# 144 unread products on 128, 64 and 32 rows behind TensorE's last product

## The chip, the cores and the metric

One core of a Trainium2 chip runs the whole kernel. The metric is the device time of one execution in microseconds. Engines are called TensorE (PE in the profile, PEld for its weight loads), VectorE (DVE), ScalarE (ACT), GpSimd (POOL) and SyncE (SP, which issues all DMAs here).

## What is computed

The reference takes x (8 x 4160 tokens of 192 numbers) through a light convolution and then through a maxout layer:

```python
w = softmax(weight_gen)                      # per token and head, 7 taps, 8 heads
x = sum over k of w[.., k] * x_pad[t + k]    # 24 columns per head
h = maximum(maximum(x @ w1, x @ w2), x @ w3) # 192 -> 768
out = h @ w_out                              # 768 -> 192
```

All is float32, and the output has 33280 rows of 192.

## The kernel before, in words

The 33280 tokens lie as 128 partitions of 260 tokens; a chunk is 4 tokens of each partition (`TC = 4`, so `CH = 512` columns on TensorE), and there are `NC = 65` chunks. For each chunk GpSimd multiplies windows of x by the softmaxed taps (`product`, line 234), VectorE adds the taps (line 263), the sums are transposed so that the 192 features lie on partitions, and `parts` (lines 311 to 328) splits them into float32r parts: `xa_hi` and `xa_lo` for the first 128 features, `xb` and `xc` for the rest. They are kept in `state["xT", c]`. The weights are split in the same way and stay in SBUF: `wa_hi`, `wa_lo`, `wb_hi`, `wb_lo`, and `wo` for the second layer.

Every product of the two layers is issued by `product_of` (line 339), at line 343. It contracts 64 rows at a time, one half of the partitions (`halves`), so that TensorE works with two row groups of 64 rows. `up` makes the upper products, 512 columns each, into a bank `ph`; `maximum` reads the bank (lines 392 and 396) and makes `h_hi` and `h_lo`. `down` multiplies `h_hi` by 384 and `h_lo` by 192 columns of `wo`, and lines 425 and 426 add the two parts of the sum into `o`.

The order is written out: a loop over chunks and 22 ticks gives the lower half's products with `lower`, and `advance_upper` puts the upper half's products between them by a count of column slots (`SLOTS`, `clock`). `plan` is a heap of later steps with the tick at which they are due. Every instruction goes through `pin`, which keeps the program's order on its engine. In the last round (`c == NC`) the second layer of the last chunk is all that is left: its sums for four tokens lie in four banks, each is finished in turn, added (`add`, line 424) and sent out alone by SyncE (line 430). Banks come from the pool `ps`: 8 buffers, each of 128 x 512 float32, handed out in turn; whoever asks for one waits for the readers of the tile that had it before.

`busy` (line 244) puts transposes into a bank that nothing reads: `k6` and `k2` in the opening make 48 of them.

The program ends with the loop over what is left in `plan`; the change adds one call behind it.

Of the kernel before, what the change touches and what calls it, by code (L numbers as in the profile page):

```python
# [13 lines left out]
F32 = mybir.dt.float32  # L14
# [7 lines left out]
P = 128  # L22
# [63 lines left out]
def lightconv_maxout_kernel(  # L86
# [11 lines left out]
    nc = tc.nc  # L98
# [7 lines left out]
    NJ = DFF // P  # L106
# [3 lines left out]
    CH = TC * P  # L110
# [25 lines left out]
    ps = ctx.enter_context(tc.tile_pool(name="ps", bufs=8, space=bass.MemoryType.PSUM))  # L136

    ident = const.tile([P, P], F32, name="ident")
    wa_hi = const.tile([P, NJ, 3, P], F32R, name="wa_hi")
# [13 lines left out]
    state = {}  # L153
# [297 lines left out]
    def lower(task, first=0, last=None):  # L451
# [7 lines left out]
        if last is None:  # L459
            settle = SETTLE if f is down and args[0] < NC - 1 else 0.0  # L460
            begun.append((clock[0] + settle, f(*args, 1)))

    words = [w.bitcast(U32) for w in (w1, w2, w3, w_out)]


# [161 lines left out]
    NC = len(chunks)  # L627
# [70 lines left out]
    for c in range(NC + 1):  # L698
        for tick in range(TICKS):
# [10 lines left out]
            k, odd = divmod(tick - (TC if tick >= 2 * DOWN_AT else 0), 2)  # L710
# [18 lines left out]
    advance_upper(float("inf"))  # L729
    while plan:  # L730
        heapq.heappop(plan)[2]()


# [32 lines left out]
```

## Time and profile before

| what | value |
|---|---|
| median of the runs | 1677.51 us (2 runs, 1677.51 to 1677.52) |
| span of the profiled execution, first to last instruction | 1676.7 us |
| TensorE products in it | 16930 |
| last product starts | 1673.22 us |
| granted TensorE clock over the span | 1.000 |

The profiled execution's own time is known by its span; the runs' median lies 0.8 us above it. Times in the rows are microseconds from the span's start. In a timeline a row that merges several instructions gives the start of the first, the time until the end of the last and their number (x2); products overlap, so the distance between starts is the pace, and a row's own length is not.

### The profile page before, as it was taken

The numbers are of one execution on the slowest core, as the hardware profiler recorded it, in microseconds if no ns is written. First come the engines' busy times: TensorE is split into PE (matmuls) and PEld (weight loads), VectorE is DVE, ScalarE is ACT, GpSimd is POOL, SyncE is SP. The second block draws the span as 40 slices with busy tenths as digits, with TensorE's granted clock in tenths as the row PEclk, the third lists the DMA queues.
The fourth block names the chain that finished last, engine by engine and source line by source line (L and its number), as shares of the span: only waits on it lengthen the run. The fifth ranks groups of instructions, "written<-read, shape, count | busy, mean of one in ns | idle before, by whom it ended". The sixth has DMA issues, their size and how long they took to land.

```text
span 1676.7 us, 42376 instructions
## 1 busy us (share of the span) xinstructions
PE 1663.2 (99%) x16930; PEld 1654.6 (99%) x16930; DVE 1106.3 (66%) x1508; ACT 1140.5 (68%) x2880; POOL 1405.2 (84%) x823
## 2 busy tenths in 40 slices
PE   7999999999999999999999999999999999999999
PEld 6999999999999999999999999999999999999999
DVE  7866666666666666666666666666666666666653
ACT  6666676676676676676676676676676676676672
POOL 7867888888898888888898888888898888888872
PEclk9999999999999999999999999999999999999999
DMA  7010101011010101011010101011010101010000
GB/s 267 11 61 21 71 11 71 36 46 71 20 62 21 71 11 71 29 53 71 20 62 20 71 11 71 23 59 71 20 62 20 71 11 71 20 61 20 21 11 30
DMA packets 20278, 79.53 MB, mean 47 GB/s; under 512 B 2296, under 2 KB 4984, under 8 KB 17392
## 3 DMA queue, kind: packets, MB, share of 16 engines
q1 hardware_dynamic: 20080, 76.83, 12.1%
q8 instruction: 132, 2.16, 0.5%
q14 instruction: 66, 0.54, 0.1%
HBM read 51.26 MB, written 25.56 MB: 46 GB/s over the span
## 4 chain that ended last, share of the span: by engine, by line
PE 98%; DMA 0%; DVE 0%; SPq 0%; POOL 0%; issue 0%; ACT 0%; DVEq 0%; POOLq 0%
PE ph L343 98%; PE ph L286 0%; DMA xt<-in_x_dram 0%; SPq L575 0%; DMA h_lo<-in_moe_w_dram 0%; POOL r L234 0%; DVE ph L518 0%; DVE ph L502 0%; PE ph L248 0%; DVE ph L525 0%; SPq L566 0%; DVE wa_lo L542 0%; ACT wa_hi L539 0%; POOL wt L205 0%; DVE w L525 0%
## 5 line engine op out<-in xcount | busy, mean ns | idle before, releaser
L234 POOL TENSOR_TENSOR r<-xt,wt 128x1344 f32<-128x1344 f32 x260 | 721.1, 2817 | 1.7 <-DMA xt<-in_x_dram 1.0
L396 DVE TENSOR_TENSOR m<-ph,m 128x512 f32<-128x512 f32 x768 | 513.0, 685 | 200.5 <-PE ph L343 113.0
L401 POOL TENSOR_TENSOR h_lo<-m,h_hi 128x512 fp32r<-128x512 f32 x378 | 488.3, 1304 | 163.9 <-ACT h_hi L399 159.2
L343 PE MATMUL ph<-xa_hi,wa_hi 64*128 64x512 f32 x2340 | 621.7, 388 | 0.0
L343 PE MATMUL ph<-xb,wb_hi 64*128 64x512 f32 x2340 | 619.8, 386 | 0.2 <-ACT xb L326 0.2
L343 PE MATMUL ph<-xa_lo,wa_hi 64*128 64x512 f32 x2340 | 619.8, 386 | 0.0
L343 PE MATMUL ph<-xa_hi,wa_lo 64*128 64x512 f32 x2340 | 619.8, 386 | 0.0
L343 PE MATMUL ph<-wo,h_hi 64*128 64x384 f32 x3120 | 590.4, 355 | 0.0
L343 PE MATMUL ph<-wo,h_lo 64*128 64x192 f32 x3120 | 550.5, 247 | 0.0
L399 ACT CAST h_hi<-m 128x512 fp32r<-128x512 f32 x378 | 234.5, 621 | 403.7 <-DVE m L396 400.7
L343 PEld LDWEIGHTS ph<-wo,h_lo 64*128 64x128 f32 x3120 | 479.3, 188 | 0.0
L343 PEld LDWEIGHTS ph<-wo,h_hi 64*128 64x128 f32 x3120 | 472.1, 184 | 0.0
L263 DVE TENSOR_REDUCE acc<-r 128x192 f32<-128x1344 f32 x252 | 389.7, 1547 | 122.2 <-POOL r L234 122.2
L308 ACT COPY room<-room 32x128 f32<-32x128 f32 x1512 | 447.9, 296 | 24.6 <-DVE room L302 6.2
L343 PE MATMUL ph<-xc,wb_lo 64*128 64x512 f32 x1170 | 451.6, 386 | 0.0
L343 PEld LDWEIGHTS ph<-xa_hi,wa_hi 64*128 64x128 f32 x2340 | 358.7, 184 | 1.6 <-issue 0.4
L343 PEld LDWEIGHTS ph<-xb,wb_hi 64*128 64x128 f32 x2340 | 356.5, 184 | 1.7 <-ACT xb L326 0.5
L343 PEld LDWEIGHTS ph<-xa_lo,wa_hi 64*128 64x128 f32 x2340 | 356.7, 184 | 1.2 <-DVE xa_lo L322 0.2
L343 PEld LDWEIGHTS ph<-xa_hi,wa_lo 64*128 64x128 f32 x2340 | 356.5, 184 | 1.4 <-issue 0.2
L392 ACT COPY m<-ph 128x512 f32<-128x512 f32 x390 | 222.0, 587 | 40.0 <-PE ph L343 35.1
L426 DVE TENSOR_TENSOR o<-ph,ob 128x192 f32<-128x192 f32 x260 | 86.5, 353 | 228.8 <-ACT ob L425 228.8
L343 PEld LDWEIGHTS ph<-xc,wb_lo 64*128 64x128 f32 x1170 | 215.3, 184 | 0.6
(74 smaller groups left out, 719.2 us busy)
## 6 DMA issues: line engine op xcount, KB each, us to landing
xt<-in_x_dram SPq DMA_DIRECT2D x20, 1728.0 KB, 6.9
out_dram<-o SPq DMA_DIRECT2D x64, 384.0 KB, 2.3
wt<-in_weight_gen_dram SPq DMA_DIRECT2D x21, 336.0 KB, 3.0
xt<-in_x_dram SPq DMA_DIRECT2D x2, 960.0 KB, 6.6
h_hi<-in_moe_w_dram SPq DMA_DIRECT2D x6, 256.0 KB, 6.3
room<-in_moe_w_out_dram SPq DMA_DIRECT2D x1, 1152.0 KB, 10.6
xt<-in_x_dram SPq DMA_DIRECT2D x1, 1152.0 KB, 5.4
h_lo<-in_moe_w_dram SPq DMA_DIRECT2D x6, 128.0 KB, 4.6
```

Source lines behind the costliest of these rows:

```text
L234: eng.tensor_tensor(to, xt[:, la + t : la + t + K].rearrange("p k (h g) -> p k h g", g=G), w.rearrange("p (h k) -> p k h", k=K) .unsqueeze ...
L263: nc.vector.tensor_reduce(state["acc", c][:, t], r, axis=AX.X, op=ALU.add)
L308: pin(nc.scalar.copy(to[:, :, p : p + 32], blocks[p : p + 32, :, f : f + 32]))
L343: ins = nc.tensor.matmul(ph[:, :n], w[h], v[h], start=begins and half == 0 and q == 0, stop=ends and half == 1 and q == len(terms) - 1,)
L392: pin(nc.scalar.copy(m, ph))
L396: pin(nc.vector.tensor_tensor(to, ph, m, op=ALU.max))
L399: later(1, lambda: pin(nc.scalar.copy(hi, to)))
L401: 2, lambda: pin(eng.tensor_tensor(lo, to, hi.bitcast(F32), op=ALU.subtract))
L426: pin(nc.vector.tensor_tensor(o[:, t], po[:, :D], ob, op=ALU.add))
```

## The change

Behind the last step of the program a new function, `after_all`, asks for banks and issues products into them. Their weights are slices of `wa_hi` and what they stream are slices of `xa_hi`, `xa_lo` and `xb` of the last chunk. Nothing reads the banks. A grid is (row groups, output columns, rounds, streamed columns): one round is one product for each row group, with a bank for each group. By the eight grids there are 10 + 32 + 16 + 18 + 32 + 8 + 12 + 16 = 144 products, and a weight load for each.

```diff
+    def after_all():
+
+        xa_hi, xa_lo, xb, xc = state["xT", NC - 1]
+        moving = (xa_hi, xa_lo, xb)
+        grids = (
+            ((128,), P, 10, (512,)),
+            ((32, 32, 32, 32), P, 8, (512,)),
+            ((64, 64), P, 8, (512,)),
+            ((64, 32, 32), P, 6, (512,)),
+            ((32, 32, 32, 32), P, 8, (384, 192)),
+            ((128,), P, 8, (384, 192)),
+            ((64, 64), 64, 6, (512,)),
+            ((64, 64), P, 8, (192,)),
+        )
+        for rows, cols, times, widths in grids:
+            banks = [ps.tile([P, CH], F32, name="ph") for _ in rows]
+            for k in range(times):
+                n = widths[k % len(widths)]
+                for r, (bank, size) in enumerate(zip(banks, rows)):
+                    h = slice(sum(rows[:r]), sum(rows[:r]) + size)
+                    pin(
+                        nc.tensor.matmul(
+                            bank[:cols, :n],
+                            wa_hi[h, k % NJ, 0, :cols],
+                            moving[k % 3][h, :n],
+                            start=True,
+                            stop=True,
+                        )
+                    )
+
...
     while plan:
         heapq.heappop(plan)[2]()
+    after_all()
```

## Rows read from the trace of the kernel before

**Rows 1.** The page: busy time, share and instructions of each engine.
```profile
PE 1663.2 (99%) x16930; PEld 1654.6 (99%) x16930; DVE 1106.3 (66%) x1508; ACT 1140.5 (68%) x2880; POOL 1405.2 (84%) x823
```

**Rows 2.** The chain that ended last, its last three pieces: start, us, what.
```profile
36.64 1636.85 PE ph L343 x15642
1673.51 0.33 ACT ob L425
1673.86 0.36 DVE o L426
```

**Rows 3.** Timeline of the end: start, us, engine, line, output<-inputs, idle before.
```profile
1665.36 0.69 DVE L396 TENSOR_TENSOR m<-ph,m 128x512 f32<-128x512 f32 x1 [0.44 <-PE ph L343]
...
1672.21 0.36 DVE L426 TENSOR_TENSOR o<-ph,ob 128x192 f32<-128x192 f32 x1 [6.16 <-ACT ob L425]
...
1672.60 1.98 SPq L430 DMA_DIRECT2D out_dram<-o  x4
...
1673.22 0.25 PE L343 MATMUL ph<-wo,h_lo 64*128 64x192 f32 x1
```

**Rows 4.** The tile o from 1660 us on: its DMAs' time to landing.
```profile
DMA to landing us min/median/max: 1.6/1.6/2.3
```

**Rows 5.** Stretches: length, busy time and instructions by engine, granted clock, DMA.
```profile
1670.00:1673.50 3.50, 3.47 (x28) 3.24 (x26) 0.93 (x3) 0.96 (x3) 0.00 (x0) 1.00 0.01 4
24.90:36.60 11.70, 11.67 (x93) 9.86 (x93) 11.49 (x24) 9.95 (x22) 10.52 (x6) 1.00 0.45 172
400.00:440.00 40.00, 40.00 (x392) 40.00 (x390) 27.69 (x37) 25.71 (x69) 34.97 (x20) 1.00 0.19 74
```

**Rows 6.** Timeline of TensorE: 512-column products, both halves of 64 rows.
```profile
1660.17 0.46 PE L343 MATMUL ph<-xa_lo,wa_hi 64*128 64x512 f32 x2
1660.40 0.46 PE L343 MATMUL ph<-xb,wb_hi 64*128 64x512 f32 x2
```

**Rows 7.** Timeline of TensorE near the start: 512-column products of one half alone.
```profile
30.16 0.39 PE L343 MATMUL ph<-xa_lo,wa_hi 64*128 64x512 f32 x1
...
30.62 0.39 PE L343 MATMUL ph<-xa_hi,wa_lo 64*128 64x512 f32 x1
```

**Rows 8.** The chain near the start: transposes of 128 rows.
```profile
26.82 1.31 PE ph L248 x12
28.12 1.53 PE ph L286 x14
```

**Rows 9.** Timeline of TensorE: 384 and 192 columns, both halves; loads of one half.
```profile
1666.18 0.33 PE L343 MATMUL ph<-wo,h_lo 64*128 64x192 f32 x2
...
1666.47 0.33 PE L343 MATMUL ph<-wo,h_lo 64*128 64x192 f32 x2
...
1668.18 0.18 PEld L343 LDWEIGHTS ph<-wo,h_hi 64*128 64x128 f32 x1
1668.29 0.19 PEld L343 LDWEIGHTS ph<-wo,h_lo 64*128 64x128 f32 x1
```

**Rows 10.** Timeline of TensorE from 64 rows to 128 and back.
```profile
32.63 0.50 PE L343 MATMUL ph<-xa_hi,wa_hi 64*128 64x512 f32 x2
32.96 0.40 PE L343 MATMUL ph<-xa_lo,wa_hi 64*128 64x512 f32 x2
...
30.94 1.49 PEld L286 LDWEIGHTS ph<-ident,r 128*128 128x128 f32 x14 [0.36 <-issue]
32.62 0.19 PEld L343 LDWEIGHTS ph<-xa_hi,wa_hi 64*128 64x128 f32 x2 [0.20 <-issue]
```

**Rows 11.** Timeline of TensorE: the two halves starting together.
```profile
36.57 0.18 PEld L343 LDWEIGHTS ph<-xa_hi,wa_hi 64*128 64x128 f32 x2 [0.20 <-issue]
36.91 0.40 PE L343 MATMUL ph<-xa_lo,wa_hi 64*128 64x512 f32 x2
```

**Rows 12.** Groups by line and shape: count, busy us, mean ns, idle before.
```profile
L286 PE MATMUL ph<-ident,r 128*64 128x128 f32 x56 | 15.0, 305 | 0.0
L248 PE MATMUL ph<-ident 128*128 128x128 f32 x48 | 5.6, 272 | 0.0
```

## The prediction

> **What bounds the kernel now.** The page's totals come first: TensorE is busy for 99% of the span and no other engine for more than 84% [rows 1]. The chain that ended last is, from 36.64 us on, one piece of 1636.85 us of line 343's products, then one ScalarE copy and one VectorE add [rows 2]. The timeline of the end shows what lies behind the last product: it starts at 1673.22, the copy of its bank at 1673.51, the add at 1673.86, ending at 1674.22, and the four output rows' DMAs are issued back to back from 1672.60 to 1674.58 [rows 2, 3]. A DMA of this tile lands 1.6 us after its issue [rows 4]. Whether that runs from the issue's start (about 1674.25) or its end, the last bytes are out at 1675.85 or 1676.2, and the span closes 0.85 or 0.5 us later, at 1676.7. So TensorE has nothing to do in the last 3.2 us, and that window is all the cover that work placed behind the last product can have. The granted clock is 1.00 (2.4 GHz) through the main stretch and through the last products, when only one half of the rows works [rows 5].
>
> **The change, grid by grid.** It removes and moves nothing; it adds 144 pairs of weight load and product at the end of TensorE's queue, and no other engine or DMA queue gets an instruction. Nothing is queued behind them. The program is over when the last engine is, so the added path counts from TensorE's next free slot, not from 1676.7.
>
> Waits: the first bank asked for is that of an upper product, whose last reader ran at 1665.36; the second grid's fourth bank and the third's two are those of the first three output sums, and the fourth grid's first is that of the last one. Their readers run from 1672.21 to 1674.22 [rows 2, 3]. By the sums below the second grid starts at about 1676, so none of these waits costs anything; the ten products of the first grid are their cover. Operands are long in SBUF.
>
> Price of a 512-column product: with both halves of 64 rows at work, successive pairs start 0.23 us apart [rows 6]; with one half alone, two steps take 0.46 us, the same 0.23 [rows 7]. The weight load is hidden in it. Alternating 384 and 192 columns take 0.29 us for the two, with both halves at work, from 1666.18 to 1666.47 [rows 9]. Two weight loads follow each other at 0.11 us at the closest [rows 9], more than 192 columns need to stream (192 / 2.4 GHz = 0.08), so a run of 192-column products costs 0.11 each.
>
> Price of 128 rows: no such product with these operands is in the trace, only transposes of 128 rows with 128 columns, 14 in 1.53 us and 12 in 1.31 us, 0.109 each [rows 8]. That is the pace of a weight load of 128 columns, so I take it as that and charge 0.23 for 512 columns and 0.29 for the 384/192 pair. If instead 0.109 were the streaming price of 128 columns on 128 rows, it would be 0.436 and 0.49: +2.1 us in the first grid and +0.8 in the sixth. The lower bound is the 512 / 2.4 GHz = 0.213 of the streaming itself: -0.2.
>
> Price of going from one row size to another: a 64-row product starts at 30.62; 14 transposes of 128 rows follow; the next 64-row product but one starts at 32.96 [rows 7, 10]. Without a cost for switching it would start at 30.62 + 0.23 + 14 x 0.109 + 0.23 = 32.61. Two switches thus cost 0.35, or 0.18 each; the weight loads show it as idle time with no releaser, 0.36 and 0.20 [rows 10]. Columns are another matter: 64- and 128-column transposes alternate within those 14 at 0.109 each [rows 8, 12], so a change in columns costs nothing.
>
> Do 32-row products run side by side? Two row groups do: two loads start within 10 ns and two products within some 14 ns of each other [rows 11]. Four at once is not in the trace. Bounds for a round of four at 512 columns: 0.23 if all run together, 0.92 if one after another. I take 0.23, since the nearest row, two groups, shows no loss at all. A middle bound is issue: the densest stretch shows eight instructions (four loads, four products) in 0.29 us, 36 ns each [rows 9]; if that were a limit, the second grid would take 2.3 us instead of 1.84, the fifth 2.3 instead of 1.16, the eighth 1.15 instead of 0.88: +1.9 in all. The Trainium skill (TensorE: Matmul & The Clock Gate, "Measured speedup vs the span model") states a 3.07-fold speedup for four groups of 32 rows at 512 columns, not four-fold. No run here shows it; by it a round would be an estimated 4 x 0.23 / 3.07 = 0.30, and the second and fifth grids together 0.9 us longer.
>
> The fourth grid (64, 32, 32) mixes sizes inside a round. Bounds: 0.23 a round if the three run together (1.38 for six), or two stages of 0.23 and a switch between any two of them: 6 x 2 x 0.23 + 11 x 0.18 = 4.74. I take 4.74, because the only changes of row size in the trace (128 to 64 and back) each cost 0.18 though they follow without any wait on another engine [rows 10]. The Trainium skill (TensorEngine Tiling (Array Packing), "Key Properties") says that a change of the tiling mode, not of the tile, drains TensorE; the rows show it for 128 against 64, none for 64 against 32.
>
> The sum: grid 1, 10 x 0.23 = 2.30; grid 2, 8 x 0.23 = 1.84; grid 3, 1.84; grid 4, 4.74; grid 5, 4 x 0.29 = 1.16; grid 6, 1.16; grid 7, 6 x 0.23 = 1.38; grid 8, 8 x 0.11 = 0.88. Together 15.30. Switches ahead of grids 1, 2, 3, 6 and 7 (grid 4 opens on 64 rows and ends on 32, as grid 5 goes on): 5 x 0.18 = 0.90. So 16.2 us of slots from 1673.22 + 0.09 = 1673.31 to 1689.5. The last 192-column product is listed at 0.25 against a slot of 0.11, so its end is at 1689.65. What follows the last work in the span was 0.5 to 0.85 us behind a DMA; behind a product I bound it by 0.2 and 0.85 and take 0.6: the span becomes 1690.2. The runs' median, 1677.51, is 0.8 above the profiled span of 1676.7, and I keep that: **1691.0 us**, 13.5 us or 0.8% slower. Of the 16.3 us that TensorE works longer, some 2.9 us are hidden beside the output's copy, add and DMA, which no longer end last.
>
> **Rivals.** (a) The mixed round runs together, 64 and 32 rows being independent groups: grid 4 costs 1.38, so 1691.0 - 3.4 = 1687.6. For it: two groups of equal size overlap fully [rows 11]. Against: every change of row size in the trace drains [rows 10].
> (b) The four groups don't all run together. In twos, grids 2 and 5 double: +3.0, 1694.0. One after another: grid 2 is 32 x 0.23 = 7.36, grid 5 16 x 0.29 = 4.64, grid 4 18 x 0.23 + 1.98 = 6.12, together +10.4, 1701.4. Against: nothing is lost with two groups; for: four have never run here.
> (c) The granted clock falls to 1.2 GHz from the fourth grid on, where TensorE drains again and again. Streaming then takes twice as long: 2.76 in grid 4 and 4.58 behind it, +7.3, 1698.3. Against: the early stretch with its drains and idle time keeps 1.00 [rows 5, 10].
> (d) Not slower: products whose bank nothing reads are left out by the build, or the end doesn't wait for them; then 1677.5 stays. This decides if no added product shows in the trace. Against it: line 248's 48 transposes write a bank that nothing reads, and all 48 ran [rows 12].
> (e) Slower by over 2%, past 1711.1: the added path would have to be 36 us, as with 32-row products one after another (26.6 us) at the low clock (twice that, some 53): about 1728.
>
> **How the numbers follow.** My forecast, with its open prices (128 rows, issue, what follows the last product): 0.58; it covers 1689.5 to 1694. (a) 0.15, (b) 0.14, (c) 0.07, (d) 0.02, (e) 0.04. The range reaches from below (a) to above (c), 1686.5 to 1699, and leaves out (d), (e) and the far end of (b). Two per cent, about what a measurement of this kernel can tell from no change, is 33.5 us: only (e) is beyond it, and nothing here removes time. Faster 0.01, within 2% 0.95, slower 0.04.
>
> **What would show it.** Up to 1673.2 the timeline should be the same, the copies and adds of the output too. Then ten 128-row products 0.23 apart, after an idle time of about 0.2 of the weight loads. In grid 2 rounds of four that start almost together and 0.23 apart; a stair of four steps of 0.23 each would speak for (b). In grid 4 two stages a round, some 0.82 us, with idle weight loads at each change; one stage of 0.23 speaks for (a). The granted clock behind 1680 decides (c). The chain should end in TensorE and not in VectorE. If the span's end isn't set by the last product, or the products before 1673 change their pace, the reasoning is wrong at its root.

## The result, and the profile after

The changed kernel takes 1694.93 us (median of two executions, 1693.72 and 1696.15) against 1677.51: a ratio of 1.0104, 95% interval 1.0074 to 1.0133. It is slower by 17.4 us, within the 2% that count as no change and within the whole range of the forecast (1686.5 to 1699), but 3.9 us above the forecast itself and above the 1689.5 to 1694 that its open prices were to cover.

The page of the changed kernel, its span and its totals, and the last two pieces of its chain in order of time:

```profile
span 1694.4 us, 42665 instructions
PE 1683.2 (99%) x17074; PEld 1668.5 (98%) x17074; DVE 1106.3 (65%) x1508; ACT 1140.7 (67%) x2880; POOL 1405.3 (83%) x823
...
35.76 1636.81 PE ph L343 x15642
1672.56 20.96 PE ph L484 x125
```

TensorE has 144 products more than in [rows 1], and VectorE, ScalarE and GpSimd have the same instructions as there. The main stretch of line 343 lasts 1636.81 us against 1636.85 in [rows 2]; it only begins 0.9 us earlier, because the opening took that much less in this execution. The end of the chain is now line 484, the added products, and the copy and add of [rows 2] are no longer in it: the last add ran beside the first added products.

The timeline of the first two grids (start, us, engine, line; x4 are four row groups merged):

```profile
1673.08 0.40 PE L484 MATMUL ph<-xb,wa_hi 128*128 128x512 f32 x1
1673.31 0.40 PE L484 MATMUL ph<-xa_hi,wa_hi 128*128 128x512 f32 x1
...
1675.02 0.19 PEld L484 LDWEIGHTS ph<-xa_hi,wa_hi 32*128 32x128 f32 x4 [0.36 <-issue]
...
1675.36 0.40 PE L484 MATMUL ph<-xa_lo,wa_hi 32*128 32x512 f32 x4
1675.59 0.40 PE L484 MATMUL ph<-xb,wa_hi 32*128 32x512 f32 x4
```

A 128-row product costs 0.23 us, as one or two halves of 64 did [rows 6, 7]. Four row groups of 32 run fully together: four loads in 0.19 us, and a round every 0.23. The idle 0.36 before the loads is the change of row size, as in [rows 10].

The mixed grid from its first round on, and behind it the sixth, both in the same execution:

```profile
1679.01 0.82 PE L484 MATMUL ph<-xa_hi,wa_hi 64*128 64x512 f32 x3
...
1680.61 0.93 PE L484 MATMUL ph<-xb,wa_hi 64*128 64x512 f32 x3
1681.04 0.18 PEld L484 LDWEIGHTS ph<-xb,wa_hi 32*128 32x128 f32 x2 [0.25 <-issue]
1681.47 0.18 PEld L484 LDWEIGHTS ph<-xa_hi,wa_hi 64*128 64x128 f32 x1 [0.25 <-issue]
1681.47 0.92 PE L484 MATMUL ph<-xa_hi,wa_hi 64*128 64x512 f32 x3
...
1682.76 0.29 PEld L484 LDWEIGHTS ph<-xa_lo,wa_hi 32*128 32x128 f32 x2 [0.25 <-issue]
1683.48 0.28 PEld L484 LDWEIGHTS ph<-xb,wa_hi 64*128 64x128 f32 x1 [0.43 <-issue]
...
1687.65 0.57 PE L484 MATMUL ph<-xb,wa_hi 128*128 128x384 f32 x1
1688.18 0.57 PE L484 MATMUL ph<-xa_lo,wa_hi 128*128 128x384 f32 x1
```

A round takes 0.86 us, two stages with an idle weight load of 0.25 ahead of each: 64 and 32 rows don't overlap. That is the cost forecast. But at 1682.8 the same load takes 0.29 instead of 0.18, the next stage comes 0.72 later instead of 0.43, and in grid 6 a pair of 384 and 192 columns takes 0.53 instead of 0.29. The table by stretches says why (the third column from the right is the granted clock):

```profile
1680.00:1682.00 2.00, 2.00 (x9) 0.84 (x8) 0.00 (x0) 0.00 (x0) 0.00 (x0) 1.00 0.00 0
1682.00:1684.00 2.00, 2.00 (x6) 0.83 (x6) 0.00 (x0) 0.00 (x0) 0.00 (x0) 0.69 0.00 0
1684.00:1686.00 2.00, 2.00 (x27) 1.80 (x30) 0.00 (x0) 0.00 (x0) 0.00 (x0) 0.50 0.00 0
...
1690.00:1692.00 2.00, 2.00 (x12) 1.08 (x10) 0.00 (x0) 0.00 (x0) 0.00 (x0) 0.50 0.00 0
1692.00:1694.00 2.00, 1.52 (x18) 1.34 (x14) 0.00 (x0) 0.00 (x0) 0.00 (x0) 0.75 0.00 0
```

From 1682.8 to 1693.0 TensorE runs at 1.2 GHz instead of 2.4. The matmul's busy column stays at 2.00 of 2.00 until the products end at 1693.5; only the clock's column and the paces show the fall.

### The profile page after: what moved, and what is told of

Same layout as the page of the kernel before. It is cut to its first block, busy times and chain, and to the rows that moved or that the text cites. A ratio compares the mean times of both kernels' runs of the same rounds, so it can differ in the third digit from the quotient of the medians.

```text
span 1694.4 us, 42665 instructions
## 1 busy us (share of the span) xinstructions
PE 1683.2 (99%) x17074; PEld 1668.5 (98%) x17074; DVE 1106.3 (65%) x1508; ACT 1140.7 (67%) x2880; POOL 1405.3 (83%) x823
## 4 chain that ended last, share of the span: by engine, by line
PE 99%; DMA 1%; SPq 0%; POOL 0%; DVE 0%; issue 0%; POOLq 0%
PE ph L343 97%; PE ph L484 1%; PE ph L286 0%; DMA xt<-in_x_dram 0%; DMA wt<-in_weight_gen_dram 0%; SPq L605 0%; POOL r L234 0%; SPq L596 0%; PE ph L248 0%; DVE ph L532 0%; POOL wt L205 0%; DVE ph L548 0%; SPq L179 0%; DVE red L190 0%; DVE den L202 0%
```

## The experiments

Each is the changed kernel with the edit shown. The kernel before ran beside them on the same chips: medians of 1677.66, 1678.09 and 1677.97 in the three sets, single executions from 1677.14 to 1680.13. Nothing reads the added banks, so leaving added products out alters no output. Each set has runs that lost the clock and runs that kept it (again and thin against sorted; thin48_dense against full_mixed; mixed12 against no_mixed), so the fall is not a matter of one chip.

**The same kernel once more (again).** No edit.

> The changed kernel once more, unaltered, for the spread of its time. Theory (the granted clock falls to 1.2 GHz in the mixed grid and stays low for most of grids 5 to 8, from a moment that differs from run to run): times differ between 1691 and 1698, by more than the 0.01 us of the two runs of the kernel before, and the profile shows a low stretch of several us behind the mixed grid. Rival (the low clock of the first profile was an accident of that one execution): the clock is 1.00 to the end, and the times lie together near 1691.

Measured: 1691.67, 1694.85, 1697.03 and 1691.70; ratio 1.0095 (1.0081 to 1.0109). The mean clocks of the four are 1.000, 0.998, 0.997 and 1.000. With the first two executions (0.999 at 1693.72, 0.997 at 1696.15) the time goes with the clock: two executions at 1.000 near 1691.7, and three at 0.997 or 0.998 between 1694.85 and 1697.03. The one at 0.999 is not settled: it has no profile, and 5 of the 33 executions of the kernel before show 0.999 too, at 1677.76 to 1680.13. The profile happened to be of one that kept the clock; its last product of line 343, its last added one, the last piece of its chain and the whole added stretch:

```profile
1672.39 0.25 PE L343 MATMUL ph<-wo,h_lo 64*128 64x192 f32 x1
...
1688.76 0.28 PE L484 MATMUL ph<-xa_lo,wa_hi 64*128 64x192 f32 x2
...
1672.64 16.39 PE ph L484 x131
...
1672.60:1689.10 16.50, 16.43 (x145) 11.02 (x144) 0.58 (x2) 0.32 (x1) 0.00 (x0) 1.00 0.08 25
```

So neither side of the expectation holds whole: the fall is no accident of one execution, and it is not in every one. Span against span, it cost 1694.4 - 1689.9 = 4.5 us in the first profile, whose main stretch began within 0.1 us of this one's.

**The mixed grid sorted (sorted).**

```diff
-            ((64, 32, 32), P, 6, (512,)),
+            ((64, 32, 32), P, 6, (512,), 1, 2),
+            ((64, 32, 32), P, 6, (512,), 0),
...
-        for rows, cols, times, widths in grids:
+        for rows, cols, times, widths, *skip in grids:
...
+                    if r in skip:
+                        continue
```

The numbers at the end of a grid are the row groups that it skips.

> The mixed grid's products in another order: six rounds of its 64-row product, then six rounds of its two 32-row products, so one change of row size instead of eleven; all 144 products stay. Theory (the changes of row size drain TensorE, and the idle time takes the clock down): grid 4 takes 2 x 1.38 + 0.2 = 2.96 us, the granted clock stays 1.00 to the end, and the time is 1689 to 1690 in every run. Rival (products on few rows take the clock down, however dense): the clock falls at about the same place, and the time is 1693 to 1697.

Measured: five executions from 1689.77 to 1690.42, clock 1.000 in each; ratio 1.0073 (1.0059 to 1.0086). The profile's stages follow each other at 0.23, with one longer step of 0.31 at the change, from 1680.86 to 1681.17; the last line is the added stretch on the chain:

```profile
1680.63 0.39 PE L487 MATMUL ph<-xa_lo,wa_hi 64*128 64x512 f32 x1
1680.86 0.39 PE L487 MATMUL ph<-xb,wa_hi 64*128 64x512 f32 x1
1681.17 0.50 PE L487 MATMUL ph<-xa_hi,wa_hi 32*128 32x512 f32 x2
...
1673.26 14.40 PE ph L487 x123
```

The same 144 products: ten changes of row size fewer are worth 1691.7 - 1690.0 = 1.7 us of the time at the full clock. The times hold the opening's scatter; the added stretches do not, and between them it is 16.39 - 14.40 = 1.99 us, 0.20 for each change. And the scatter up to 1697 is gone.

**Changes of row size with all rows at work (alt128).**

```diff
-            ((64, 32, 32), P, 6, (512,)),
+            *(g for _ in range(6) for g in (((128,), P, 1, (512,)), ((64, 64), P, 1, (512,)))),
```

> In place of the mixed grid, six times a 128-row product and then a pair of 64-row products, all of 512 columns: the same twelve stages and eleven changes, but no 32-row product. Theory (any change of row size drains): stages 0.43 us apart, idle weight loads of some 0.25 at each change, the clock falls in this grid as in the changed kernel; 1692 to 1698. Rival (it is 32-row products, or sizes mixed within one half of the rows, that cost): stages 0.23 apart or the clock 1.00; 1688 to 1691.

Measured: 1692.01. The weight loads stand as in the mixed grid, 0.43 apart with 0.25 idle, but the clock column stays at 1.00:

```profile
1679.45 0.19 PEld L484 LDWEIGHTS ph<-xa_hi,wa_hi 64*128 64x128 f32 x2 [0.24 <-issue]
1679.89 0.19 PEld L484 LDWEIGHTS ph<-xa_hi,wa_hi 128*128 128x128 f32 x1 [0.25 <-issue]
...
1679.00:1684.50 5.50, 5.50 (x24) 2.51 (x26) 0.00 (x0) 0.00 (x0) 0.00 (x0) 1.00 0.00 0
```

The half of the theory on drains holds (changes between 128 and 64 rows cost the same idle time), the half on the clock misses: that idle time did not take it down here. One execution can be luck; full_mixed below settles it.

**Few rows without a change (thin).**

```diff
-            ((64, 32, 32), P, 6, (512,)),
+            ((32,), P, 24, (512,)),
```

> In place of the mixed grid, 24 products of 512 columns on the first 32 rows alone, one after another without a change of row size. Theory (idle time takes the clock down, not few rows): 0.23 us each, 5.5 us in all, granted clock 1.00 to the end; about 1692. Rival (few rows at work take the clock down): the clock falls to 0.5 during these 24 or just behind them, and the time is 1697 or more.

Measured: 1697.88, and the clock falls at 1683.0, 3.1 us behind the start of the first of the 24:

```profile
1679.97 0.49 PE L484 MATMUL ph<-xa_hi,wa_hi 32*128 32x512 f32 x1
...
1682.62 0.38 PE L484 MATMUL ph<-xb,wa_hi 32*128 32x512 f32 x1
1682.84 0.46 PE L484 MATMUL ph<-xa_hi,wa_hi 32*128 32x512 f32 x1
1683.11 0.62 PE L484 MATMUL ph<-xa_lo,wa_hi 32*128 32x512 f32 x1
1683.53 0.62 PE L484 MATMUL ph<-xb,wa_hi 32*128 32x512 f32 x1
...
1679.00:1683.00 4.00, 4.00 (x23) 2.99 (x20) 0.00 (x0) 0.00 (x0) 0.00 (x0) 1.00 0.00 0
1683.00:1686.50 3.50, 3.50 (x10) 2.63 (x9) 0.00 (x0) 0.00 (x0) 0.00 (x0) 0.50 0.00 0
```

The theory falls. Within the 24 there is no idle time, products come every 0.23 us, and the clock goes down all the same. What this fall shares with the one in the mixed grid is few rows at work: 32 in each product here, 64 and idle time in each stage there. That is the new theory.

**The same changes of row size, all rows at work, 32-row products among them (full_mixed).**

```diff
-            ((64, 32, 32), P, 6, (512,)),
+            *(g for _ in range(6) for g in (((64, 64), P, 1, (512,)), ((32, 32, 32, 32), P, 1, (512,)))),
```

> In place of the mixed grid, six times a pair of 64-row products and then four 32-row products, all of 512 columns: its twelve stages and eleven changes of row size, but all 128 rows at work in each stage. Theory (the clock falls where few rows of the array work over several us, by few rows in a stage or by idle time between stages or both): stages 0.43 us apart as in the mixed grid, the clock 1.00 to the end, 1691 to 1692.5 in every run. Rival (the idle time of the changes alone takes the clock down, and the one look at 128 and 64 rows was luck): a spread up to 1694 to 1697, as with the unaltered change.

Measured: five executions from 1691.37 to 1692.98, clock 1.000 in each; ratio 1.0083 (1.007 to 1.0097).

```profile
1679.47 0.19 PEld L484 LDWEIGHTS ph<-xa_hi,wa_hi 64*128 64x128 f32 x2 [0.24 <-issue]
1679.91 0.19 PEld L484 LDWEIGHTS ph<-xa_hi,wa_hi 32*128 32x128 f32 x4 [0.25 <-PE ph L484]
...
1678.70:1684.10 5.40, 5.40 (x50) 2.61 (x50) 0.00 (x0) 0.00 (x0) 0.00 (x0) 1.00 0.00 0
```

Eleven changes between the very sizes of the mixed grid, with the same idle 0.25, and with twice as many rows at work in each stage the clock stays.

**Half of the rows without a change (half).**

```diff
-            ((64, 32, 32), P, 6, (512,)),
+            ((64,), P, 24, (512,)),
```

> In place of the mixed grid, 24 products of 512 columns on the first 64 rows alone, one after another. Theory (32 rows alone are too few and 64 rows without idle time are enough, as in the products ahead of 1673): 0.23 us each, clock 1.00 to the end, 1692 to 1693.5 in every run. Rival (half of the rows is few enough): the clock falls in or behind these 24, 1696 or more.

Measured: 1694.21, 1692.64, 1693.40 and 1692.68, clock 1.000 in each. The first lies above the expected 1693.5; its main stretch began only at 37.61 us, the latest of all profiles. That line of the chain, and the stretch of the 24:

```profile
37.61 1636.84 PE ph L343 x15932
...
1680.90:1686.50 5.60, 5.60 (x30) 4.29 (x27) 0.00 (x0) 0.00 (x0) 0.00 (x0) 1.00 0.00 0
```

**When the clock comes back (thin48_dense).** Grids 4 to 8 are left out.

```diff
-            ((64, 32, 32), P, 6, (512,)),
-            ((32, 32, 32, 32), P, 8, (384, 192)),
-            ((128,), P, 8, (384, 192)),
-            ((64, 64), 64, 6, (512,)),
-            ((64, 64), P, 8, (192,)),
+            ((32,), P, 48, (512,)),
+            ((128,), P, 40, (512,)),
```

> Grids 1 to 3, then 48 products on 32 rows alone, then 40 products on all 128 rows, all of 512 columns; grids 4 to 8 are left out. Both low stretches seen so far lasted 10.2 us, one of them across a dense grid on 128 rows. Theory A (the clock stays low as long as few rows work or the row size keeps changing, and rises some us into a dense stretch): low from about 1683 to the end of the 48, 0.43 us a product, and back at 1.00 within 5 us of the 40; about 1710. Theory B (a low stretch lasts about 10 us whatever is done): the clock rises near 1693 while the 32-row products still run; about 1706.

Measured: 1712.25. Before the fall, the rest of the 48, the first and the later products on 128 rows:

```profile
1679.00:1682.40 3.40, 3.40 (x18) 2.49 (x15) 0.00 (x0) 0.00 (x0) 0.00 (x0) 1.00 0.00 0
1682.60:1697.90 15.30, 15.30 (x37) 11.25 (x35) 0.00 (x0) 0.00 (x0) 0.00 (x0) 0.50 0.00 0
1698.00:1702.70 4.70, 4.70 (x12) 3.73 (x12) 0.00 (x0) 0.00 (x0) 0.00 (x0) 0.50 0.00 0
1703.00:1709.50 6.50, 6.50 (x30) 5.10 (x28) 0.00 (x0) 0.00 (x0) 0.00 (x0) 1.00 0.00 0
```

Theory A holds, though the time is 2 us above its estimate: the low stretch is 20 us long here, and ends 4.9 us into the work on all rows (1697.96 to about 1702.9). A fall is paid for by what comes behind it too.

**The first grid alone (first_only).** The lines of grids 2 to 8 are taken out.

> Only grid 1 is left of the change: ten products on 128 rows behind the last product; grids 2 to 8 are left out. Theory (2.5 us of added products lie beside the output's copy, add and DMA): TensorE's last product ends near 1676, the span stays at 1676.7 to 1677, and the time is that of the kernel before within 0.4 us. Rival (whatever TensorE does behind its last product is added to the time): 2.5 us slower.

Measured: 1678.12 (eleven executions), against 1678.09 for the kernel before beside it: ratio 1.0000 (0.9991 to 1.0009). The last add and the last added product:

```profile
1673.41 0.36 DVE L426 TENSOR_TENSOR o<-ph,ob 128x192 f32<-128x192 f32 x1 [0.21 <-ACT ob L425]
...
1675.15 0.40 PE L477 MATMUL ph<-xa_hi,wa_hi 128*128 128x512 f32 x1
```

TensorE's last product ends at 1675.55, the span at 1676.4: ten products, 2.5 us, cost nothing behind the last sum because the output's path is as long.

**Twelve rounds (mixed12).**

```diff
-            ((64, 32, 32), P, 6, (512,)),
+            ((64, 32, 32), P, 12, (512,)),
```

> The mixed grid with 12 rounds instead of 6, nothing else altered. Theory (few rows at work, seen over several us, take the clock down; six rounds are so short that some executions end them at 1.00): the clock falls in every execution, the rounds behind the fall take 1.44 us instead of 0.86, and every time is 1702 to 1709. Rival (the fall is a matter of chance in any execution and not of this grid's length): some times at 1696 to 1698, the value with the clock at 1.00 throughout (six more rounds of 0.86 on 1691.7).

Measured: four executions from 1702.05 to 1703.35, clock 0.996 or 0.997 in each; ratio 1.0145 (1.013 to 1.0161). None is near 1697. The grid's first round, and the stretches before and behind the fall:

```profile
1678.89 0.81 PE L484 MATMUL ph<-xa_hi,wa_hi 64*128 64x512 f32 x3
...
1679.00:1683.90 4.90, 4.90 (x20) 2.02 (x17) 0.00 (x0) 0.00 (x0) 0.00 (x0) 1.00 0.00 0
1684.20:1692.00 7.80, 7.80 (x20) 3.11 (x23) 0.00 (x0) 0.00 (x0) 0.00 (x0) 0.50 0.00 0
1692.00:1697.50 5.50, 5.50 (x46) 4.74 (x48) 0.00 (x0) 0.00 (x0) 0.00 (x0) 0.50 0.00 0
```

With 12 rounds all four executions fall, with 6 rounds three of six for certain. In the two profiles with a fall in this grid it came 3.8 and 5.2 us after the grid's first product (1679.0 to 1682.8; 1678.9 to 1684.1), and six rounds at the full clock last 4.6. That fits executions which are through before the fall; the moment itself was seen in these two only.

**Without the mixed grid (no_mixed).** Its line is taken out.

> The mixed grid is left out, 126 products stay. Theory (it alone takes the clock down, and at 1.00 it costs 4.6 us from its first product to the next grid's): clock 1.00 to the end, 1686.5 to 1688.5 in every run. Rival (another grid, that of 64 rows and 64 columns or that of 192 columns, takes it down too): a spread up to 1692.

Measured: five executions from 1686.87 to 1687.57, clock 1.000 in each; ratio 1.0054 (1.0041 to 1.0066). The added stretch on its chain:

```profile
1673.27 11.66 PE ph L483 x119
```

By the two added stretches grid 4 costs 16.39 - 11.66 = 4.73 us at the full clock, the 4.74 of the sum; by the times it is 1691.7 - 1687.3 = 4.4, with the opening's scatter and two chips in it. In the median of the first two executions it costs 1694.9 - 1687.3 = 7.6.

## Why the prediction was right, and where it was not

The measured time lies in the range because the range reached up to rival (c), not because the forecast's own sum gave it: two executions at the full clock agree with the sum, and the rest is the step that failed, the chance of (c).

*What bounds the kernel, and the cover.* Right. The chain ends in TensorE, and all but 2.3 us of the added path count: counted from the start of the main stretch, the last product starts 16.35 us later in again than before, and the span ends 14.0 us later (1689.9 - 35.83 against 1676.7 - 36.64). The prediction said 2.9. first_only shows the cover: 2.5 us of products behind the last one change nothing.

*The prices at the full clock.* Right, against the execution of again that kept it. From the last product of line 343 to the end of the last added one the sum had 1689.65 - 1673.22 = 16.43 us; measured 1688.76 + 0.28 - 1672.39 = 16.65. Most of the 0.22 too much lies in the mixed rounds, 0.86 each against the sum's 0.82: a change there costs 0.20, not 0.18. Of the open prices, 128 rows cost 0.23 for 512 columns and not 0.436; four groups of 32 run fully together (0.23, not 0.92); and in grid 5 sixteen instructions in 0.285 us show that 36 ns each is no limit of issue. For a round of four the sum's 0.23 was right. The estimate of 0.30 by the Trainium skill (TensorE: Matmul & The Clock Gate, "Measured speedup vs the span model") is not borne out in this steady stream, and the measurement decides. The Trainium skill's rule on drains (TensorEngine Tiling (Array Packing), "Key Properties") is borne out for 64 against 32 rows by the idle 0.25 ahead of each stage. Rival (a) is out: 0.20 a change by sorted, and 0.86 a round by the timeline where (a) needs 0.23.

*What follows the last product.* The estimate of 0.6 us was small: 1689.9 - 1689.04 = 0.86, at the upper bound.

*The time outside the span.* Wrong by 1.0, cancelled by an opposite error. I set the profiled span of 1676.7 against another execution's 1677.51 and got 0.8. In every execution of the three sets, the kernel before among them, time and span differ by 1.8 (1677.66 and 1675.9; 1691.67 and 1689.9). The profiled execution of before was therefore itself some 1 us longer than the median. The opening is where it can be: the main stretch began at 36.64 us there and in all profiles between 35.44 and 37.61, while its length differs by less than 0.1 us. That scatter is the kernel's own noise of 1 to 2 us.

Together, +0.22 (sum), +0.26 (end), +1.0 (outside) and -0.83 (last product at 1672.39 instead of 1673.22) make 1691.0 into 1691.65; the two executions at the full clock took 1691.67 and 1691.70. That the last two nearly cancel is no luck: the forecast added its 13.5 us to the median of the runs, which the late opening of one profile does not move.

*Rival (c), the clock.* This step failed: the chance of 0.07, and its argument "the early stretch with its drains and idle time keeps 1.00". It happened in three of six executions for certain and in a fourth, at 0.999, perhaps. In the profiled one it cost 4.5 us; in the other of the first two, 2.0 us above 1691.7, the opening's scatter may have a part. It was named, with the right place, and its price of 7.3 us was too large, since the fall came 3.8 us into the grid and ended before the last products. The argument took idle time alone for the cause. In the early stretch all or half of the rows worked between a few changes; in the mixed grid a stage works on 64 rows and there is a change in every 0.43 us. The runs part the two: the same eleven changes with 128 rows at work keep 1.00 in all six executions (alt128, full_mixed), 64 rows without a change keep it (half, sorted), 32 rows without a change lose it (thin, thin48_dense), and so does the mixed grid if it lasts (mixed12). On 32 rows alone that rests on one execution each of thin and thin48_dense. The Trainium skill (TensorE: Matmul & The Clock Gate, "HAM oscillation — how this bites in real kernels") puts a fall down to stretches in which TensorE waits. No such wait stands ahead of the falls here: the clock fell with gaps of 0.25 us in the mixed grid, and in thin without any within the 24.

*Rivals (b), (d), (e).* Out: the groups run together, all 144 products are in the trace, and the clock fell without serial products.

*Left open.* Whether it is the rows themselves that count or something that goes with them, and what sets the delay of the rise: counted from the start of the grid behind the few rows, 4.9 us in thin48_dense, 6.0 in mixed12 (1691.8 to 1697.8), 6.7 in thin (1686.5 to 1693.2), 8.8 in the first profile (1684.2 to 1693.0). The grids between differ in rows, columns and changes, and no run here takes these apart.

## What to carry to other kernels

Price TensorE's tail by slots (columns and changes of row size), not by listed durations, and first ask how long the output's path behind the last product is: that much is free. Group products of one row size: a change cost 0.2 us here. Many changes with 64 rows at work, or 32 rows alone without a change, also put the clock at stake, for 10 to 20 us in these profiles. A time that scatters by several us between executions while the profile's busy share stays full is a reason to read the clock in stretches.

## What the runs showed of the hardware that was not expected

A TensorE that is 100% busy by the profile can lose its clock: 24 products on 32 rows, 0.23 us apart without a pause, fell to 1.2 GHz 3.1 us after their start (thin), 24 on 64 rows did not (half). And the fall outlived the few rows by 5 to 9 us of further work in the four profiles where that can be read.
